# Accumulating the output products before normalizing, in the same step of an attention and MLP block

## The chip, the cores and the metric

The kernel runs on one core of one Trainium2 chip. The metric is the device time of one execution, in microseconds (us). The engines of the core are TensorE (PE: matrix products, with weight loads shown as PEld), VectorE (DVE), ScalarE (ACT), GpSimd (POOL) and SyncE (SP, which issues most DMAs). Each runs its own instructions in the order in which the program issues them; they wait for one another by semaphores.

## What is computed

One transformer block with modulated layer norms, in float32. The part that matters:

```python
h = _layernorm(x) * (1 + ca) + sa
# A: attention over the last W = 512 cached keys, 32 query heads, 16 kv heads
q = h @ wq
scores = einsum("bhqd,bhkd->bhqk", q, k) * Dh ** -0.5
o = einsum("bhqk,bhkd->bhqd", softmax(scores), v)
x = x + ga * (o @ wo)
h = _layernorm(x) * (1 + cb) + sb
# B: MLP
x = x + gb * ((silu(h @ w1) * (h @ w3)) @ w2)
```

There are 2048 rows of x, a width of 576, a head size of 128 and an MLP width of 4608.

## The kernel before

Each float32 operand of a product is split into two float16 halves, high and low, and a product is made of three: high by high, high by low, low by high. The MLP uses a fast scheme with seven products in place of eight; its weights are made ready in the background during the attention stage, by small tasks with due times.

**Slots.** The attention stage is a loop over 128 slots `i`, one for each pair of a query head and a block of 512 rows, and inside it over four tiles `t` of 128 rows. A slot's work is spread over several passes of the loop. In pass `i`, at tile `t`, the program issues:

- `scores(i, t)`: three products (L483) into a bank `pss`; VectorE then takes the maximum (L487) and scales it (L488) for ScalarE's exponential, `weights(i, t)` (L500), whose end frees the bank;
- `turn_away`, `half_high` and `half_low`: the exponentials of tiles 0 to 2 are split by ScalarE (L532) and GpSimd (L537) and turned by a transposing DMA (L544). Tile 3 is turned on TensorE instead (`turn`, L523), and its halves come from ScalarE (`turn_high`, L527, at t = 1 of the next pass) and VectorE (`turn_low`, L552, at t = 2);
- `query(i + 1, t)`: a third of the next slot's query products (L410, L414), which ScalarE (L467) and VectorE (`query_low`, L473) split;
- after the four tiles, `values(i - 1)`: twelve products (L562) of the turned weights with the values. The first two need only high halves of the weights, the third needs the low half of all four tiles.

**Normalizing.** `normalize(i - 2)` (L571) is one VectorE instruction at t = 1. It multiplies the value products `po` by the reciprocals of the row sums `r`, which arrive by DMA, into a buffer `on` that shares three places with other tiles. `split_on(i - 2)` makes its halves at t = 3 (L581 on ScalarE, L582 on GpSimd).

**Output products.** Two slots (the two query heads of one kv head) make a pair. `attend_out(pair, t, j, ...)` multiplies the outputs of one tile by the output weights: six products (L433) for j = 0, six more for j = 1, into one accumulator `E`, two PSUM banks wide and single. With j = 1, VectorE adds the result to the running rows (`acc`, L592, "the accumulate"). The table `outs` lays these out one call a tile, so that in the steady state the call with j = 1, and its accumulate, falls on t = 1 and t = 3 of each pass, and the first products of the next result (j = 0) on t = 2 and t = 0.

**Small sums in E.** The background tasks find peaks of weights. A tiny product (L310, L1135, L1167) sums a peak over partitions into columns 400 to 415 of E's second bank, and a small VectorE copy takes it out (L315, L1141, L1170). These are the tasks `("total", t)` and `("taken", t)` of a step; totals are issued just ahead of the accumulate, copies after it, on odd steps.

**Order.** The schedule is manual: on every engine the instructions run in program order. At t = 1, VectorE therefore has the maximum and its scaling, normalize, the accumulate, copies if any, the step's tasks (peak searches such as L305, L1126 and L1162, gates, statistics), and then the next tile's maximum and turn_low.

**Factors of activations.** `act_factors(lo, hi, piece)` (L1180) turns peaks of weights into the scale factors of the MLP's activations, in five pieces of a few instructions on at most 28 columns, called once near the end of the attention stage and once early in the MLP stage, one piece a step.

Of the kernel before, what the change touches and what calls it, by code (L numbers as in the profile page):

```python
# [38 lines left out]
G = NF // 2  # L39
# [9 lines left out]
def tile_block(  # L49
# [35 lines left out]
    def t_bank():  # L85
        return tpool.tile([P, 512], F32, tag="T", name="pt")

    def half_split(a):
        return a.rearrange("p (a n) -> p a n", a=2)
# [338 lines left out]
    def back(ps, o, w, t, first, last):  # L428

        rows = slice(t * P, (t + 1) * P)  # L430
        for n, (x, y) in enumerate(((0, 0), (0, 1), (1, 0))):
            for h in range(2):
                nc.tensor.matmul(  # L433
                    ps[:, h, :HALF],
                    o[:, x, rows],
                    w[:, y, h * HALF : (h + 1) * HALF],
                    start=first and n == 0,
                    stop=last and n == 2,
                )
# [11 lines left out]
    n = len(slots)  # L451
# [19 lines left out]
    def query_low(i):  # L471
        q, ps = state[i]["qT"], state[i].pop("q")
        nc.vector.scalar_tensor_tensor(q[:, 1], ps, Q_DOWN, q[:, 0], op0=ALU.mult, op1=ALU.subtract)  # L473
# [43 lines left out]
    def turn(i, t):  # L517

        st = state[i]
        p = st.pop(("p", t))  # L520
        ps = st["t"] = t_bank().rearrange("p (j n) -> p j n", j=KC)
        for j in range(KC):
            nc.tensor.transpose(ps[:, j, :], p[:, j * P : (j + 1) * P], ident)  # L523
# [5 lines left out]
    def half_high(i, t):  # L529

        hp = state[i]["hp", t] = pool.tile([P, 2, SB], F16, tag="hf", name="hp", bufs=HF)
        nc.scalar.copy(hp[:, 0, :], state[i]["p", t])  # L532

    def half_low(i, t):

        hp = state[i]["hp", t]
        nc.gpsimd.tensor_sub(hp[:, 1, :], state[i].pop(("p", t)), hp[:, 0, :])  # L537

    def turn_away(i, t):

        if t == 0:
            state[i]["pt"] = pool.tile([P, 2, KC, SB], F16, tag="pt", name="ptw")
        pt = state[i]["pt"]
        nc.sync.dma_start_transpose(  # L544
            out=pt.rearrange("p x c n -> p (x c) n")[:, :, t * P : (t + 1) * P],
            in_=state[i].pop(("hp", t)).rearrange("p x k -> p (x k)"),
        )

    def turn_low(i, t):
        cols = slice(t * P, (t + 1) * P)  # L550
        pt = state[i]["pt"]
        nc.vector.tensor_sub(pt[:, 1, :, cols], state[i]["t"], pt[:, 0, :, cols])  # L552
# [14 lines left out]
    def normalize(i):  # L567
        st = state[i]
        po = st.pop("po")
        on = st["on"] = pool.tile([P, SB], F32, tag="raw", name="on", bufs=RB)  # L570
        nc.vector.tensor_mul(  # L571
            on.rearrange("d (t p) -> d t p", t=ST),
            po.rearrange("d (t p) -> d t p", t=ST),
            st["r"].rearrange("d p t -> d t p"),
        )
# [8 lines left out]
    def attend_out(pair, t, j, total):  # L584
        u, _, b = slots[2 * pair]
        lane[0] += j == 0
        ps = spare()
        back(ps, state[2 * pair + j]["o"], wos[u][:, j], t, j == 0, j == 1)
        if j == 1:
            run(*total)  # L590
            a = half_split(acc[b][:, t, :])
            nc.vector.scalar_tensor_tensor(  # L592
                a, ps[:, :, :HALF], factors[:, uses[u][0], 2:3], a, op0=ALU.mult, op1=ALU.add
            )
# [453 lines left out]
    def at(i, t, task, *args):  # L1048

        tasks.setdefault((i, t), []).append((task, args))  # L1050

    def run(i, t):
        for task, args in tasks.pop((i, t), ()):
            task(*args)
# [20 lines left out]
    def scale_cols(kind, ps, small, down):  # L1075

        nc.tensor.matmul(ps[:, :P], ones, spreads.pop(kind)[:, :P], start=True, stop=True)
        nc.vector.tensor_reduce(small[:, 2:3], ps[:, :P], axis=AX.X, op=ALU.max)
        powers(small, small[:, 2:3], 0, 1, 5, down)
        for v in (vecs["shift", kind], vecs["gain", kind]):  # L1080
            nc.vector.tensor_scalar(v, v, small[:, 10:11], None, op0=ALU.mult)
# [27 lines left out]
    out_down, acts_down = table[:, 2 * NF : 2 * NF + G + 1], table[:, 2 * NF + G + 1 : 2 * NF + 2 * G + 2]  # L1109
# [8 lines left out]
    def spare():  # L1118
        return lane[1][lane[0] % 2] if lane[1] else E
# [60 lines left out]
    def act_factors(lo, hi, piece):  # L1180

        top, h_down = mlp_small[:, 2:3], mlp_small[:, 5:6]
        both = stats.rearrange("p (g j) k -> p g j k", j=2)[:, lo:hi]
        downs, pairs = both[:, :, :, 0], both[:, :, :, 1]
        a = acts_down[:, lo:hi]
        if piece == 0:
            nc.vector.tensor_max(a, pairs[:, :, 0], pairs[:, :, 1])
            nc.vector.tensor_scalar(a, a, top, 2.5 * D * 2.0**-13.5, op0=ALU.mult, op1=ALU.mult)
        elif piece == 1:
            nc.vector.tensor_scalar(a, a, top, 2.0**-60, op0=ALU.mult, op1=ALU.max)  # L1190
            d = in_down[:, 2 * lo : 2 * hi]
            nc.vector.tensor_scalar(d, d, h_down, None, op0=ALU.mult)
        elif piece < 4:
            j = piece - 2
            nc.vector.reciprocal(pairs[:, :, j], a)
            nc.vector.tensor_mul(pairs[:, :, j], pairs[:, :, j], downs[:, :, j])
        else:
            if hi == G:
                hi += 1
                nc.vector.tensor_copy(acts_down[:, G : G + 1], acts_down[:, G - 1 : G])  # L1200
            d = out_down[:, lo:hi]
            nc.vector.tensor_scalar(d, d, mlp_gate_down, None, op0=ALU.mult)
            nc.vector.tensor_mul(d, d, acts_down[:, lo:hi])

    def find(into, u, k, *key):
# [52 lines left out]
    def step_at(step, task, *args):  # L1258
        at(step // ST, step % ST, task, *args)
# [78 lines left out]
    def late_at(step, task, *args):  # L1338
        at(("m", step // len(ORDER)), step % len(ORDER), task, *args)

    turns = len(items[ITEMS:]) // 4
    for late in range(turns):
# [15 lines left out]
            plan += [(step, make, number + k, maker, w, k), (step + STORE, store_now, number + k)]  # L1358
        for step, task, *args in plan:
            late_at(total + step, task, *args)  # L1360
    for piece in range(5):
        late_at(2 * len(ORDER) * turns + len(ORDER) + 1 + piece, act_factors, (NF - FEW) // 2, G, piece)
    for k, (i, t) in enumerate(((n - 4, 0), (n - 4, 2), (n - 3, 0), (n - 2, 0))):
        at(i, t, load_wset, 0, k)
# [81 lines left out]
    for c in range(3):  # L1446
        i = 117 + 3 * c
# [47 lines left out]
    at(109, 2, make_cols, "gain", "b", 4, 1.0, "T")  # L1495
    at(109, 3, lambda: spread_peaks("b", mlp_small))
    at(110, 1, lambda: scale_cols("b", t_bank(), mlp_small, 2.0**-8))
    for piece in range(5):
        step_at(ST * (n - 4) + 2 + piece, act_factors, 0, (NF - FEW) // 2, piece)
    for b in (2, 3):  # L1500
        for t in range(ST):
# [62 lines left out]
    for i in range(n + 2):  # L1564
        run(i, -1)
        for t in range(ST):
            if t > 1 and i < n:
                turn_away(i, t - 2)
            if t == 0 and 1 <= i <= n:
                turn_away(i - 1, 2)  # L1570
            slot, tile = (i - 1 if t == 1 else n, ST - 1)
            if 0 <= slot < n:
                turn(slot, tile)
            if i < n:
                scores(i, t)
            if 2 <= i <= n and t == 1:
                normalize(i - 2)
            if 1 <= i <= n and t == 2:
                turn_low(i - 1, ST - 1)
                if i == n:  # L1580
                    turning.close()
                    after = ctx.enter_context(tc.tile_pool(name="after", bufs=1, space=PSUM))
                    lane[1] = (E, after.tile([P, 2, 512], F32, tag="T2", name="pf"))
            if t == 3 and i + 1 < n:
                query_low(i + 1)
            if i < n:
                weights(i, t)
            if t < 3 and i < n:
                half_high(i, t)
                half_low(i, t)  # L1590
            if t == 1 and 1 <= i <= n:
                turn_high(i - 1, ST - 1)
            if 1 <= i <= n and t < 2:
                sums(i - 1, t)
            if 2 <= i <= n and t == 3:
                split_on(i - 2)
            if i + 1 < n and t < ST - 1:
                query(i + 1, t)
            if i >= m0:
                for _ in range(3 if (i, t) == (n + 1, 0) else 1):  # L1600
                    next(stream)
            for piece in outs.get((i, t), ()):
                attend_out(*piece, (i, ("total", t)))
            run(i, ("total", t))
            run(i, ("taken", t))
            run(i, t)
            if 1 <= i <= n and t == 2:
                sums(i - 1, t)
            run(i, t)
        if 1 <= i <= n:  # L1610
            values(i - 1)
        if i == n:
            normalize(n - 1)
            split_on(n - 1)
# [73 lines left out]
```

## Time and profile before

| | us |
|---|---|
| three runs | 2758.09, 2758.36, 2758.54 (median 2758.36) |
| profiled execution, its own time | 2758.39 |
| span of its instructions | 2756.2 |
| attention with running slots, window 97 to 1622: PE busy | 1495.1 of 1525.0 |
| same window: DVE, ACT, POOL busy | 1170.9, 1137.4, 1188.9 |
| MLP, window 1622 to 2757: PE busy | 1123.4 of 1135.0 |

The mean granted TensorE clock is 0.995. Busy time is the union of an engine's instructions; an engine that waits for a semaphore is idle. In the lines of the trace, `L592` is line 592 of the kernel, `acc<-pe,factors,acc` names what an instruction writes and reads, `[1.01 <-POOL o L582]` is idle time before it and what ended it. The rows of time are: start in us from the span's start, duration in us, engine, line, operation, tiles, shapes, count.

### The profile page before, as it was taken

The numbers are of one execution on the slowest core, as the hardware profiler recorded it, in microseconds if no ns is written. First come the engines' busy times: TensorE is split into PE (matmuls) and PEld (weight loads), VectorE is DVE, ScalarE is ACT, GpSimd is POOL, SyncE is SP. The second block draws the span as 40 slices with busy tenths as digits, with TensorE's granted clock in tenths as the row PEclk, the third lists the DMA queues.
The fourth block names the chain that finished last, engine by engine and source line by source line (L and its number), as shares of the span: only waits on it lengthen the run. The fifth ranks groups of instructions, "written<-read, shape, count | busy, mean of one in ns | idle before, by whom it ended". The sixth has DMA issues, their size and how long they took to land. (4 is left out here: it accounts for less than half of the span.)

```text
span 2756.2 us, 44751 instructions
## 1 busy us (share of the span) xinstructions
PE 2685.1 (97%) x15406; PEld 1512.8 (55%) x15406; DVE 1997.3 (72%) x3555; ACT 1617.8 (59%) x3013; POOL 1881.1 (68%) x1748
## 2 busy tenths in 40 slices
PE   6899999999999999999999999999999999999998
PEld 3455555555555555555555555555555555555555
DVE  7877788877788787877876667777766656666666
ACT  5777778777777877777677735544443333333332
POOL 5577788888788977877669637688873465333435
PEclk8999999999999999999999999999999999999999
DMA  5778888778786887989889945656643444333332
GB/s 186 171 178 193 194 182 188 175 176 189 169 185 166 190 196 180 214 181 210 192 189 208 256 131 171 200 167 200 210 149 108 161 121 128 103 102 111 104 107 87
DMA packets 593460, 463.84 MB, mean 168 GB/s; under 512 B 442704, under 2 KB 472528, under 8 KB 592208
## 3 DMA queue, kind: packets, MB, share of 16 engines
q1 hardware_dynamic: 592944, 460.69, 65.5%
q8 instruction: 121, 1.98, 0.3%
q14 instruction: 107, 0.88, 0.1%
q10 hardware_dynamic: 288, 0.30, 0.0%
HBM read 264.19 MB, written 95.99 MB: 131 GB/s over the span
## 5 line engine op out<-in xcount | busy, mean ns | idle before, releaser
L537 POOL TENSOR_TENSOR hp<-p,hp 128x512 f16<-128x512 f32 x384 | 449.6, 1173 | 266.3 <-ACT hp L532 143.8
L500 ACT ACTIVATE p<-pss,table,factors 128x512 f32<-128x512 f32 x512 | 396.9, 775 | 354.9 <-DVE table L488 182.5
L849 PEld LDWEIGHTS <-wset 128*128 128x128 f16 x3528 | 344.5, 98 | 337.4 <-issue 4.4
L487 DVE TENSOR_REDUCE table<-pss 128x1 f32<-128x512 f32 x512 | 350.5, 685 | 206.0 <-PE pss L483 202.0
L849 PE MATMUL py<-hset,wset 128*128 128x512 f16 x2016 | 483.1, 380 | 0.0
L433 PE MATMUL pe<-o 128*128 128x288 f16 x3024 | 453.1, 286 | 10.1 <-DVE acc L592 9.6
L483 PE MATMUL pss<-k,qT 128*128 128x512 f16 x1536 | 418.8, 380 | 14.2 <-ACT p L500 10.4
L433 PEld LDWEIGHTS <-o 128*128 128x128 f16 x3072 | 300.5, 98 | 184.5 <-issue 15.7
L562 PE MATMUL po<-ptw,v 128*128 128x512 f16 x1536 | 358.2, 381 | 8.2 <-DMA ptw<-hp 4.1
L849 PE MATMUL px<-hset,wset 128*128 128x512 f16 x1512 | 361.5, 379 | 1.6 <-ACT p L500 1.6
L94 POOL TENSOR_TENSOR akv<-u,akv 128x512 f16<-128x512 f32 x141 | 165.0, 1180 | 179.2 <-ACT akv L93 171.4
L410 PE MATMUL pq<-hT,wq 128*128 128x512 f16 x1092 | 282.3, 381 | 1.8 <-POOL hT L252 1.1
L532 ACT CAST hp<-p 128x512 f16<-128x512 f32 x384 | 237.3, 618 | 13.2 <-POOL hT L256 0.6
L562 PEld LDWEIGHTS <-v 128*128 128x128 f16 x1536 | 147.8, 98 | 172.8 <-issue 16.2
L483 PEld LDWEIGHTS <-qT 128*128 128x128 f16 x1536 | 147.8, 98 | 129.2 <-issue 15.5
L934 PEld LDWEIGHTS <-akv 128*128 128x128 f16 x1728 | 169.0, 98 | 89.3 <-issue 0.8
L592 DVE SCALAR_TENSOR_TENSOR acc<-pe,factors,acc 128x576 f32<-128x576 f32 x252 | 204.6, 812 | 4.3 <-PE pe L433 4.3
L582 POOL TENSOR_TENSOR o<-on,o 128x512 f16<-128x512 f32 x128 | 150.3, 1174 | 54.0 <-ACT o L581 51.9
L410 PEld LDWEIGHTS <-wq 128*128 128x128 f16 x1092 | 107.2, 98 | 128.5 <-issue 2.9
L928 DVE SCALAR_TENSOR_TENSOR acc<-pf,table,acc 128x576 f32<-128x576 f32 x140 | 113.5, 811 | 80.8 <-PE pf L934 80.8
L1027 ACT COPY u<-py 128x512 f32<-128x512 f32 x72 | 42.2, 586 | 202.1 <-PE py L849 200.2
L1020 ACT ACTIVATE s<-s,table 128x512 f32<-128x512 f32 x72 | 52.0, 722 | 176.3 <-DVE s L1019 176.3
(246 smaller groups left out, 4793.8 us busy)
## 6 DMA issues: line engine op xcount, KB each, us to landing
wset<-wd SPq DMA_DIRECT2D x213, 320.0 KB, 3.2
r<-row SPq DMA_DIRECT2D x128, 256.0 KB, 3.9
oset<-od SPq DMA_DIRECT2D x106, 288.0 KB, 3.2
wraw<-in_w SPq DMA_DIRECT2D x36, 768.0 KB, 5.4
wd<-wmade SPq DMA_DIRECT2D x75, 320.0 KB, 3.3
wset<-wd SPq DMA_DIRECT2D x71, 160.0 KB, 2.2
w2raw<-in_w SPq DMA_DIRECT2D x19, 576.0 KB, 5.2
wd<-ring SPq DMA_DIRECT2D x33, 320.0 KB, 2.9
```

The lines of the kernel that those rows point to most:

```text
L94: eng.tensor_sub(halves[:, 1], src, halves[:, 0])
L410: nc.tensor.matmul(ps, w[:, k // 2, m, :], hT[:, DC + m if k == 1 else m, :], start=s == 0, stop=False)
L433: nc.tensor.matmul(ps[:, h, :HALF], o[:, x, rows], w[:, y, h * HALF : (h + 1) * HALF], start=first and n == 0, stop=last and n == 2,)
L483: nc.tensor.matmul(pss, q[:, x, rows], k[:, y, :], start=n == 0, stop=n == 2)
L487: nc.vector.tensor_reduce(nm[:, 0:1], pss, axis=AX.X, op=ALU.max, negate=True)
L500: nc.scalar.activation(p, pss, AF.Exp, bias=nm[:, 1:2], scale=factor, accum_out=st["l"][:, t : t + 1])
L532: nc.scalar.copy(hp[:, 0, :], state[i]["p", t])
L537: nc.gpsimd.tensor_sub(hp[:, 1, :], state[i].pop(("p", t)), hp[:, 0, :])
L562: nc.tensor.matmul(po, v[:, x, c, :], pt[:, y, c, :], start=c == 0 and n == 0, stop=c == KC - 1 and n == 2)
L592: nc.vector.scalar_tensor_tensor(a, ps[:, :, :HALF], factors[:, uses[u][0], 2:3], a, op0=ALU.mult, op1=ALU.add)
L849: nc.tensor.matmul(ps, w[:, a, :], h[:, b, :], start=start and n == 0, stop=stop and n == 6, skip_group_check=True)
L934: nc.tensor.matmul(ps[:, h, :HALF], a[:, rows], w[:, b, :], start=m == 0, stop=m == 2)
```

## The change

Two things change. First, at t = 1 the call of `normalize(i - 2)` moves within the same step: from right behind the scores to behind the step's `attend_out` calls. On VectorE it thus goes from ahead of the accumulate to behind it, still ahead of the copies ("taken") and of the step's tasks. Second, the last piece of `act_factors` is cut in two, so that its final product comes one step later; the two places that schedule the pieces count to six.

```diff
         elif piece < 4:
...
-        else:
+        elif piece == 4:
             if hi == G:
                 hi += 1
                 nc.vector.tensor_copy(acts_down[:, G : G + 1], acts_down[:, G - 1 : G])
             d = out_down[:, lo:hi]
             nc.vector.tensor_scalar(d, d, mlp_gate_down, None, op0=ALU.mult)
+        else:
+            hi += hi == G
+            d = out_down[:, lo:hi]
             nc.vector.tensor_mul(d, d, acts_down[:, lo:hi])
...
-    for piece in range(5):
+    for piece in range(6):
         late_at(2 * len(ORDER) * turns + len(ORDER) + 1 + piece, act_factors, (NF - FEW) // 2, G, piece)
...
-    for piece in range(5):
+    for piece in range(6):
         step_at(ST * (n - 4) + 2 + piece, act_factors, 0, (NF - FEW) // 2, piece)
...
             if i < n:
                 scores(i, t)
-            if 2 <= i <= n and t == 1:
-                normalize(i - 2)
             if 1 <= i <= n and t == 2:
...
             for piece in outs.get((i, t), ()):
                 attend_out(*piece, (i, ("total", t)))
+            if 2 <= i <= n and t == 1:
+                normalize(i - 2)
             run(i, ("total", t))
             run(i, ("taken", t))
             run(i, t)
```

## The prediction

> **What bounds the kernel now.** First the page: busy time by engine.
>
> ```profile
> PE 2685.1 (97%) x15406; PEld 1512.8 (55%) x15406; DVE 1997.3 (72%) x3555; ACT 1617.8 (59%) x3013; POOL 1881.1 (68%) x1748
> ```
>
> TensorE (PE) is the bound; its idle time is 2756.2 - 2685.1 = 71 us. VectorE (DVE) has slack on average, but the change touches only steps of the attention stage, so the second view is who TensorE waited for (us in total, times, longest):
>
> ```profile
> PE pe L433 <- DVE acc L592: 9.6, 10, 2.4
> ```
> ```profile
> PE po L562 <- DVE ptw L552: 3.2, 7, 0.7
> ```
> L433 are the output products into the one accumulator E; L592 reads E out ("accumulate"); L552 (turn_low) makes the low half of the turned weights of tile 3, which the third value product (L562) of the same slot needs; L315, L1141 and L1170 are small copies of peaks out of a corner of E. Third, the VectorE and TensorE timelines of the longest of the ten waits (start us, us, engine, line, what; in brackets the idle time before and who ended it):
>
> ```profile
> 581.83 1.06 DVE L571 TENSOR_TENSOR on<-po,r 128x512 f32<-128x512 f32 x1 [2.94 <-DMA r<-row]
> 582.80 0.81 DVE L592 SCALAR_TENSOR_TENSOR acc<-pe,factors,acc 128x576 f32<-128x576 f32 x1
> 583.53 0.68 DVE L305 TENSOR_REDUCE top<-kvraw 128x1 bf16<-128x512 f32 x1
> ```
> ```profile
> 583.67 0.90 PE L433 MATMUL pe<-o 128*128 128x288 f16 x6 [2.43 <-DVE acc L592]
> ```
>
> The multiplication L571 (normalize) waited 2.94 us for its DMA, and the accumulate, whose products were long complete, stood behind it; TensorE then waited for E. All ten waits are of this kind, at t = 1 (the others mostly await a buffer). The change removes this order.
>
> **What the swap does to an ordinary step.** Most steps look like this one:
>
> ```profile
> 1000.44 0.21 DVE L488 TENSOR_SCALAR table<-table,factors 128x1 f32<-128x1 f32 x1
> 1000.57 1.09 DVE L571 TENSOR_TENSOR on<-po,r 128x512 f32<-128x512 f32 x1
> 1001.57 0.82 DVE L592 SCALAR_TENSOR_TENSOR acc<-pe,factors,acc 128x576 f32<-128x576 f32 x1
> 1002.29 0.69 DVE L487 TENSOR_REDUCE table<-pss 128x1 f32<-128x512 f32 x1
> 1003.02 0.21 DVE L488 TENSOR_SCALAR table<-table,factors 128x1 f32<-128x1 f32 x1
> 1003.20 0.69 DVE L552 TENSOR_TENSOR ptw<-pt,ptw 128x512 f16<-128x512 f32 x1
> ```
> ```profile
> 1000.59 0.90 PE L433 MATMUL pe<-o 128*128 128x288 f16 x6
> ...
> 1002.84 0.90 PE L433 MATMUL pe<-o 128*128 128x288 f16 x6
> ...
> 1004.96 2.75 PE L562 MATMUL po<-ptw,v 128*128 128x512 f16 x12
> ```
>
> VectorE is ready at 1000.57, while TensorE completes E only at 1000.59 + 0.90 = 1001.49. Today the multiplication fills just that hole. Swapped, the accumulate cannot start before 1001.49: VectorE idles 0.92 us, is free 0.72 later (1002.29 - 1001.57) at 1002.21, and the multiplication holds it for another 1.00 (1001.57 - 1000.57) to 1003.21 instead of 1002.29. **All that is queued behind it on VectorE comes 0.92 later**: the maximum of tile 2, L552, and any small copies and peak searches of the step. E itself is free earlier by 0.08 only, and TensorE wanted it at 1002.84 anyway. Here it costs nothing: L552 would end at 1004.81, and the third value product starts two spacings of some 2.75/12 = 0.23 after 1004.96, at 1005.4: 1.5 us of slack before, 0.6 after. Most slots of the VectorE timeline have this hole. Normalize issues this one instruction and no DMA, so the queues of SP and GpSimd keep their order; its reader, split_on, comes two tiles later, and the bank of po that it frees is written again by the next slot's value products only.
>
> **Term 1, the waits that go.** Eight of the ten go whole: 9.6 - 2.43 - 2.01 = 5.2 us. The long ones are the wait at 583.67 and this one, behind which the windows view (stretch, its length, busy time of each engine, granted clock, DMA share, GB/s) has a stretch at half clock:
>
> ```profile
> 966.32 0.90 PE L433 MATMUL pe<-o 128*128 128x288 f16 x6 [2.01 <-DVE acc L592]
> ```
> ```profile
> 967.80:971.00 3.20, 3.20 (x14) 1.57 (x13) 2.43 (x6) 2.30 (x5) 0.69 (x1) 0.50 1.54 144
> ```
>
> At 581.83 the multiplication still waits for its DMA, so what follows comes only the accumulate's 0.73 (583.53 - 582.80) earlier. TensorE, freed 2.43 earlier, is stopped again by L552, which is late next: 0.7 is kept. At 966.32, 3.20 us at a granted clock of 0.50 are a loss of 1.6 that goes too; of these 3.6 about 1.6 is kept, for the same reason (0.7, and 0.9 that the half clock cost before L552 was asked for). Term 1: -(5.2 + 0.7 + 1.6) = **-7.5** (if all were kept: -11.2).
>
> **Term 2, the small copies out of E.** In 36 of the steps a copy stands behind the accumulate, first and last:
>
> ```profile
> 109.36 0.15 DVE L315 COPY us<-pe 128x1 f32<-128x1 f32 x1
> ```
> ```profile
> 1461.08 0.15 DVE L1170 COPY table<-pe 128x1 f32<-128x1 f32 x1
> ```
> ```profile
> 436.67 1.08 DVE L571 TENSOR_TENSOR on<-po,r 128x512 f32<-128x512 f32 x1
> 437.67 0.82 DVE L592 SCALAR_TENSOR_TENSOR acc<-pe,factors,acc 128x576 f32<-128x576 f32 x1
> 438.40 0.15 DVE L1141 COPY table<-pe 128x2 f32<-128x2 f32 x1
> ```
> ```profile
> 436.69 0.90 PE L433 MATMUL pe<-o 128*128 128x288 f16 x6
> ...
> 438.99 0.90 PE L433 MATMUL pe<-o 128*128 128x288 f16 x6
> ```
>
> The copy is issued by the step's "taken" tasks, which the multiplication now precedes. New order: E complete 437.59, accumulate, multiplication at 438.32, copy at 439.32 to 439.47. Does the next output product wait for the copy? It reads other columns of E, and whether it must can be seen where a copy comes late:
>
> ```profile
> 1170.36 0.17 DVE L315 COPY us<-pe 128x1 f32<-128x1 f32 x1
> ```
> ```profile
> 1170.59 0.90 PE L433 MATMUL pe<-o 128*128 128x288 f16 x6 [0.18 <-DVE us L315]
> ```
>
> The product starts 0.06 after the copy's end: it waits. So at 438.99 it would start at 439.52, 0.54 late. By the same working 29 of the 36 steps lose 0.5 to 0.6 (0.56 on average, 16.2) and seven, where VectorE has little or no hole, 1.0 together: **+17.2**. Below, if copies do not hold TensorE: 0.
>
> The Trainium skill's page "PSUM — Partial Sum Buffer" (section "PSUM bank collisions raise a hardware error") says that two engines' accesses are to be ordered by bank and quadrant, not by address, even for disjoint columns; by that rule the copies hold the product and the sum keeps this term, while by addresses alone it would end 17.2 lower. The row at 1170.59 agrees with the rule.
>
> **Term 3, L552 late.** With a reduction or two between accumulate and L552, the slack of the step at 1000 is gone:
>
> ```profile
> 391.32 1.35 DVE L1162 TENSOR_REDUCE peak_cols<-w2raw 128x1 bf16<-128x1152 f32 x1
> ...
> 393.43 0.68 DVE L552 TENSOR_TENSOR ptw<-pt,ptw 128x512 f16<-128x512 f32 x1
> ```
> ```profile
> 394.17 2.32 PE L562 MATMUL po<-ptw,v 128*128 128x512 f16 x10 [0.15 <-DVE ptw L552]
> ```
>
> L552 already ends (394.11) where TensorE waits for it, so the whole 0.93 becomes a wait. Taking 0.93 less the slack in each step without a copy (and less what L552 itself waits for ScalarE): five steps have none left (4.6), five have 0.3 to 0.65 (2.6), eight about 0.7 (2.0), eight nearly enough (0.5): 9.7. The L552 of the first and the last of these 26:
>
> ```profile
> 212.04 0.68 DVE L552 TENSOR_TENSOR ptw<-pt,ptw 128x512 f16<-128x512 f32 x1
> ```
> ```profile
> 1558.05 0.68 DVE L552 TENSOR_TENSOR ptw<-pt,ptw 128x512 f16<-128x512 f32 x1
> ```
>
> In the copy steps, already held 0.55, another 2.5. Term 3: **+12.2**.
>
> **Other.** Exponentials of tile 2 come up to 0.9 later, hence the buffers of the scores that they release, the qT halves and the transposing DMAs behind them. The nearest row:
>
> ```profile
> PE pss L483 <- ACT p L500: 10.4, 15, 2.5
> ```
>
> If these 15 waits grow by half of 0.92 each, 7 us come on top; if TensorE, held elsewhere in the same steps, finds half of them done, 5 go. I take 0, between the two. The sixth piece only moves a product of a few columns one step on, twice:
>
> ```profile
> L1203 DVE TENSOR_TENSOR table<-table 128x5 f32<-128x5 f32 x1 | 1.2, 1194 | 0.0
> ```
>
> Nothing reads it so soon; VectorE's own slack there hides it (between -1.2 and +1.2 without that cover): 0.
>
> **Sum.** -7.5 + 17.2 + 12.2 = +21.9. The profiled execution took 2758.39 us (its span 2756.2 and 2.2 around it), 0.03 from the median of 2758.36: **2780.3**, say 2780.
>
> **Rivals.** (a) *Faster*: VectorE's idle share covers the hole and only the waits go. That needs L552 to have over 0.93 us of slack nearly everywhere and copies that do not hold E: 2758.4 - 11.2 = 2747. For it: 28% idle VectorE, and 1.5 us of slack in the step at 1000. Against: 394.17 and 1170.59. The Trainium skill's "Perfetto Trace Analysis" (section "Optimization Strategy") advises to find what the busiest engine's gaps wait for and to start that sooner; followed blindly it gives this rival. (b) *Copies free*: the product at 1170.59 was held by something that ended with the copy. Then 2758.4 - 7.5 + 12.2 = 2763. (c) *No change in effect*: holes and waits cancel, within 2753 to 2763; needs half of term 3 absorbed as well as (b). (d) *Worse*: the chain behind the later exponentials adds its 7, 2787 and over.
>
> **Chances.** Forecast 0.70, (a) 0.08, (b) 0.12, (c) 0.05, (d) 0.05. A measurement tells 0.2% (5.5 us) from no change. (b) lies at that edge: 0.07 within, 0.05 slower. Slower 0.70 + 0.05 + 0.05 = 0.80, same 0.05 + 0.07 = 0.12, faster 0.08. The range runs from (b), 2763, to (d), 2788.
>
> **What would show it.** Right: waits of L433 for L592 nearly gone; new waits of L433 for L1141, L1170 and L315, some 30 of half a us; waits of L562 for L552 up from 3.2 to about 12; VectorE idling before L592 for TensorE, many times the 4.3 of today:
>
> ```profile
> DVE acc L592 <- PE pe L433: 4.3, 3, 3.0
> ```
>
> Wrong: L433 starting before the copy has ended (term 2), or L552 no later relative to the value products (term 3).

## The result, and the profile after

The changed kernel takes 2784.08 us (median of five runs, 2783.5 to 2789.65) against 2758.54 for the kernel before on the same chip: a ratio of 1.0095, 95% interval 1.0081 to 1.0109. That is 25.5 us slower by the medians and 26.2 (22.3 to 30.1) by the ratio, which is not that of the medians. The prediction was 2780, 21.9 slower than its base.

The profiled execution of the changed kernel took 2789.65 us, 5.6 above its median; its rows are read as what happens, and sizes are taken from the timed runs. The page, span and busy time by engine:

```profile
span 2787.8 us, 44802 instructions
...
PE 2694.9 (97%) x15406; PEld 1512.9 (54%) x15406; DVE 1998.9 (72%) x3555; ACT 1617.7 (58%) x3013; POOL 1877.4 (67%) x1748
```

TensorE runs the same 15406 products and is the bound as before. The windows view of the two kernels, each with the attention stage to its last output product and with the rest (stretch, its length, busy time of PE, PEld, DVE, ACT and POOL, granted clock, DMA share, GB/s), before:

```profile
97.00:1622.00 1525.00, 1495.14 (x8592) 839.72 (x8590) 1170.91 (x2355) 1137.42 (x2202) 1188.91 (x1126) 1.00 0.82 189
1622.00:2756.00 1134.00, 1123.38 (x6527) 637.72 (x6525) 752.56 (x1041) 423.90 (x710) 638.97 (x562) 1.00 0.44 139
```

and after:

```profile
97.00:1655.90 1558.90, 1505.61 (x8590) 840.25 (x8588) 1173.45 (x2355) 1136.93 (x2201) 1185.33 (x1126) 1.00 0.81 184
1655.90:2787.80 1131.90, 1121.71 (x6527) 637.07 (x6525) 751.52 (x1040) 423.84 (x710) 638.66 (x562) 1.00 0.44 139
```

The attention stage grew by 33.9 us, the rest shrank by 2.1: all of the loss is made where the instructions were swapped. That PE's busy time grows by 10.5 with the same products is in part a matter of reading. Neighbouring rows of PE overlap by some 0.16 us (below, 443.00 + 0.90 = 443.90, while its successor in the trace starts at 443.74), and a row that had to wait doesn't, so each wait is some 0.1 to 0.16 longer than the idle time in its row. The stage has 82 rows that waited where it had 42, which makes 4 to 6 of the 10.5; the rest stays open.

Whom TensorE waited for after (us in total, times, longest):

```profile
PE po L562 <- DVE ptw L552: 13.3, 23, 1.8
PE pss L483 <- ACT p L500: 11.8, 13, 2.5
PE pe L433 <- DVE table L1141: 6.1, 15, 0.5
PE pe L433 <- DVE us L315: 5.5, 12, 0.5
...
PE pe L433 <- DVE table L1170: 2.2, 5, 0.5
```

The row of 9.6 us in which L433 waited for L592 is gone. In its place stand 32 waits of L433 for the small copies, none over 0.5, together 13.8, and every one of these products starts 0.05 to 0.06 after the copy's end; and the waits of L562 for L552 rose from 3.2 to 13.3. Whom VectorE waited for after:

```profile
DVE acc L592 <- PE pe L433: 75.4, 87, 3.2
...
DVE acc L592 <- PE pe L1135: 11.8, 13, 0.9
DVE acc L592 <- PE pe L310: 11.8, 13, 0.9
...
DVE acc L592 <- PE pe L1167: 2.7, 3, 0.9
```

The hole before the accumulate, three waits and 4.3 us before, is now met 87 times for L433, and 29 times more where the small sum is the last product into E. The copy step that the prediction worked out (436.67 to 438.99 before), now on VectorE and on TensorE:

```profile
443.98 0.82 DVE L592 SCALAR_TENSOR_TENSOR acc<-pe,factors,acc 128x576 f32<-128x576 f32 x1 [0.92 <-PE pe L1135]
444.72 1.07 DVE L571 TENSOR_TENSOR on<-po,r 128x512 f32<-128x512 f32 x1
445.70 0.16 DVE L1141 COPY table<-pe 128x2 f32<-128x2 f32 x1
```
```profile
443.00 0.90 PE L433 MATMUL pe<-o 128*128 128x288 f16 x6
...
445.92 0.90 PE L433 MATMUL pe<-o 128*128 128x288 f16 x6 [0.45 <-DVE table L1141]
```

VectorE idles 0.92, the copy ends at 445.86, and 0.06 later the next output product starts: 2.92 after the one before it, where it was 2.30 (436.69 to 438.99). That is 0.62 late; the prediction had 0.54. And the third value product of the step that stood at 394.17, with no slack; the output product ahead of it before, then the same product and the value product after:

```profile
391.27 0.90 PE L433 MATMUL pe<-o 128*128 128x288 f16 x6
```
```profile
396.62 0.90 PE L433 MATMUL pe<-o 128*128 128x288 f16 x6
...
400.49 2.32 PE L562 MATMUL po<-ptw,v 128*128 128x512 f16 x10 [0.75 <-DVE ptw L552]
```

In its row the wait grows from 0.15 to 0.75. Counted from that output product it starts 3.87 later instead of 2.90 (391.27 to 394.17): 0.97 late, where the prediction had 0.93. The row understates it, since the small sum ahead of it (L1167) came late too, without a row of its own.

### The profile page after: what moved, and what is told of

Its sections match the earlier page's. It is cut to its first block, busy times and chain, and to the rows that moved or that the text cites. A ratio compares the mean times of both kernels' runs of the same rounds, so it can differ in the third digit from the quotient of the medians.

```text
span 2787.8 us, 44802 instructions
## 1 busy us (share of the span) xinstructions
PE 2694.9 (97%) x15406; PEld 1512.9 (54%) x15406; DVE 1998.9 (72%) x3555; ACT 1617.7 (58%) x3013; POOL 1877.4 (67%) x1748
## 5 line engine op out<-in xcount | busy, mean ns | idle before, releaser
L500 ACT ACTIVATE p<-pss,table,factors 128x512 f32<-128x512 f32 x512 | 396.9, 775 | 386.5 <-DVE table L488 220.4
L433 PE MATMUL pe<-o 128*128 128x288 f16 x3024 | 453.2, 286 | 13.9 <-DVE table L1141 6.1
L483 PE MATMUL pss<-k,qT 128*128 128x512 f16 x1536 | 418.5, 380 | 15.5 <-ACT p L500 11.8
L433 PEld LDWEIGHTS <-o 128*128 128x128 f16 x3072 | 300.9, 98 | 192.3 <-issue 23.7
L562 PE MATMUL po<-ptw,v 128*128 128x512 f16 x1536 | 364.0, 382 | 23.4 <-DVE ptw L552 13.3
L592 DVE SCALAR_TENSOR_TENSOR acc<-pe,factors,acc 128x576 f32<-128x576 f32 x252 | 204.8, 813 | 102.3 <-PE pe L433 75.4
L562 PEld LDWEIGHTS <-v 128*128 128x128 f16 x1536 | 147.8, 98 | 194.5 <-issue 36.4
L483 PEld LDWEIGHTS <-qT 128*128 128x128 f16 x1536 | 148.1, 98 | 130.4 <-issue 16.8
```

What stands on the lines that cost most here:

```text
L433: nc.tensor.matmul(ps[:, h, :HALF], o[:, x, rows], w[:, y, h * HALF : (h + 1) * HALF], start=first and n == 0, stop=last and n == 2,)
L483: nc.tensor.matmul(pss, q[:, x, rows], k[:, y, :], start=n == 0, stop=n == 2)
L500: nc.scalar.activation(p, pss, AF.Exp, bias=nm[:, 1:2], scale=factor, accum_out=st["l"][:, t : t + 1])
L562: nc.tensor.matmul(po, v[:, x, c, :], pt[:, y, c, :], start=c == 0 and n == 0, stop=c == KC - 1 and n == 2)
L592: nc.vector.scalar_tensor_tensor(a, ps[:, :, :HALF], factors[:, uses[u][0], 2:3], a, op0=ALU.mult, op1=ALU.add)
```

## The experiments

The question was not whether these waits exist but what each is worth, and whether the terms of the sum are independent. Each kernel was timed beside the kernel before on its chip; its time against before is (ratio - 1) x 2758.4, with the interval of the ratio. The trace of the changed kernel shows 124 swapped steps: 36 with a copy, the 26 of term 3, the ten waits and 52 others (texts below that were written before their runs count 53 of these). The edits choose in which steps normalize goes behind the accumulate, by a condition `last`:

```diff
-            if 2 <= i <= n and t == 1:
+            last = ...
+            if 2 <= i <= n and t == 1 and not last:
                 normalize(i - 2)
...
             for piece in outs.get((i, t), ()):
                 attend_out(*piece, (i, ("total", t)))
+            if 2 <= i <= n and t == 1 and last:
+                normalize(i - 2)
```

| kernel | normalize behind the accumulate in | median us | ratio, 95% interval | us against before |
|---|---|---|---|---|
| copy_steps | the 36 steps with a copy | 2777.16 | 1.007, 1.0057 to 1.0084 | +19.3 |
| plain_steps | all steps without one | 2767.66 | 1.0033, 1.0021 to 1.0045 | +9.1 |
| copies_first | all, and behind the copies too | 2780.28 | 1.0077, 1.0064 to 1.0091 | +21.2 |
| copy_behind | the copy steps, behind the copies too | 2770.82 | 1.005, 1.0038 to 1.0062 | +13.8 |
| late_low | the 26 steps of term 3 | 2769.92 | 1.0046, 1.0034 to 1.0058 | +12.7 |
| ten_waits | the ten steps whose wait goes | 2756.33 | 0.9992, 0.9984 to 1.0001 | -2.2 |
| free_steps | the 52 other plain steps | 2763.21 | 1.0022, 1.0012 to 1.0032 | +6.1 |
| free_early | 23 of these | 2760.14 | 1.0007, 0.9998 to 1.0015 | +1.9 |
| free_late | 29 of these | 2762.08 | 1.0018, 1.0009 to 1.0026 | +5.0 |
| tile_earlier | the ten; elsewhere a tile earlier | 2759.9 | 1.001, 1.0002 to 1.0019 | +2.8 |
| pieces_only | none; the sixth piece alone | 2756.54 | 0.9999, 0.9991 to 1.0008 | -0.3 |

**Copy steps alone**, `last = (i, ("taken", 1)) in tasks`:

> Normalize behind the accumulate only in the steps that have a copy out of E (36 with running output products); the factors stay in five pieces. Theory (three terms: waits that go, copies that hold TensorE, turn_low late): only the copy steps pay, 17.2 for the late copies and 2.5 for turn_low, no wait goes: 2758.5 + 19.7 = 2778. Rival (copies are free, the hole in VectorE costs the same in every step): 36 of 122 steps pay 36/122 of the 25.5 us measured, 2766.

+19.3. Its waits:

```profile
PE pe L433 <- DVE acc L592: 9.4, 10, 2.4
PE pe L433 <- DVE table L1141: 6.4, 15, 0.5
PE pe L433 <- DVE us L315: 5.5, 12, 0.5
PE po L562 <- DVE ptw L552: 5.3, 12, 0.7
...
PE pe L433 <- DVE table L1170: 2.5, 5, 0.6
```

All of the copies' waits are here, with the ten old ones still in place. The size is that of term 2 and the copy steps' share of term 3 (17.2 + 2.5).

**Steps without a copy alone**, `last = (i, ("taken", 1)) not in tasks`:

> Normalize behind the accumulate only in the steps without a copy; five pieces. Theory: -7.5 for the waits of the accumulate that go, +9.7 for turn_low late: 2761, with no wait of L433 for a copy beyond those of before. Rival (copies free): 86 of 122 steps pay 18 us, 2776.

+9.1, well over the +2.2 expected. Whether the ten waits give back less or the other steps cost more, this run alone can't tell; the later ones ask for each part.

```profile
PE po L562 <- DVE ptw L552: 10.5, 17, 1.8
```

**Copies ahead of normalize.** If the copies are what costs, taking them out of normalize's way should give most of it back:

```diff
             run(i, ("total", t))
             run(i, ("taken", t))
+            if 2 <= i <= n and t == 1:
+                normalize(i - 2)
             run(i, t)
```

> The changed kernel, but with normalize behind the copies too, still ahead of the step's other tasks: E is free right after accumulate and copy. Theory: the 17.2 us of the copies go, turn_low in those steps has less cover and takes back up to 3: 2784 - 17.2 + 0 to 3 = 2767 to 2770; waits of L433 for copies below 1 us. Rival (copies free): nothing changes, 2784.

A miss: +21.2 (17.7 to 25.1), only 5.0 less than the change's 26.2, where some 15 were expected. The copies' waits are gone, but

```profile
PE po L562 <- DVE ptw L552: 19.4, 30, 1.8
PE pss L483 <- ACT p L500: 14.5, 19, 2.5
```

L552, which the prediction had late by 2.5 us in the copy steps, is now late in many of them. So the terms are not independent: while a copy holds TensorE, VectorE gets on towards L552. To price that by itself, the same in the copy steps only:

> Only the 36 copy steps are swapped, and in them the multiplication goes behind the accumulate and the small copies. Theory: the copies no longer hold the next output product (its 33 waits for L1141, L315 and L1170, 20.4 us worked out from TensorE's timeline when these steps alone were swapped, go to none), but L552 now shows its whole delay: 0.93 less its slack adds up to some 10 us in these steps instead of the 2.5 that were left beside the held product. So about +10 against before, 2769, of which the hold is worth some 9 of the +18 that these steps cost with the copies behind. Rival one: L552 alone is not late enough, and taking the copies out of the way frees nearly all: +2.5, 2761. Rival two: the later exponentials that follow from the hole, not the copies, are what costs: as slow as with the copies behind, 2777, with waits for L500 above 14 us.

+13.8 against +19.3 with the copies behind: the hold is worth 5.5, near the 5.0 of the pair before (26.2 - 21.2), though in both pairs the intervals overlap, and most of the rest is L552, whose row was 3.2 in the kernel before:

```profile
PE po L562 <- DVE ptw L552: 12.1, 19, 1.0
```

The expectation, which put some 10 on L552, comes nearest of the three. One step shows the exchange. With normalize ahead of the copy, TensorE and then VectorE:

```profile
456.28 0.90 PE L433 MATMUL pe<-o 128*128 128x288 f16 x6 [0.46 <-DVE us L315]
...
458.39 2.32 PE L562 MATMUL po<-ptw,v 128*128 128x512 f16 x10
```
```profile
458.02 0.68 DVE L552 TENSOR_TENSOR ptw<-pt,ptw 128x512 f16<-128x512 f32 x1
```

and with the copy first:

```profile
457.55 1.24 PE L562 MATMUL po<-ptw,v 128*128 128x512 f16 x5 [0.87 <-DVE ptw L552]
```
```profile
456.81 0.68 DVE L552 TENSOR_TENSOR ptw<-pt,ptw 128x512 f16<-128x512 f32 x1
```

In the first the output product waits 0.46 for the copy and L562 for nothing; in the second nothing holds the output product, and L562 starts 0.06 after L552's end at 457.49, having waited 0.87.

**The 26 steps of term 3 alone,** `last` by a list of their passes:

> Normalize behind the accumulate only in the 26 steps without a copy in which turn_low was reckoned to come late; five pieces. Theory (each step costs 0.93 less its slack): 9.7 over the kernel before, 2759 + 10 = 2769. Rival (the hole in VectorE costs the same in every step, 25.5 / 122 = 0.21): 2759 + 5.4 = 2764.5.

+12.7, on the theory's side. Its waits for L552:

```profile
PE po L562 <- DVE ptw L552: 8.3, 13, 1.8
```

These rows grew by 5.1, less than the time, since they leave out short waits and the overlap. The length of a pass doesn't: from the start of the first value product (L562) at the end of one pass to that at the end of the next. Its usual length is the median over the profiles in which neither this pass nor the one before was changed. The 26 passes and those right behind them, without the ten waits' passes and those right behind these, are 41; together they took 11.5 us longer than usual here, near the 9.7 of the theory, and 10.9 in plain_steps.

**The ten waits alone,** `last = i in (6, 36, 37, 44, 68, 69, 76, 84, 121, 124)`:

> Normalize behind the accumulate only in the ten steps in which TensorE waited for the accumulate before; five pieces. Theory: the waits go, of the two long ones 0.7 and 1.6 us are kept: 2758.5 - 7.5 = 2751. Rival (what TensorE is freed from it meets again at turn_low or at the transposing DMA in all ten): 2758. Second rival (all 9.6 and the stretch at half clock are kept): 2747.

-2.2 (-4.4 to +0.3), a miss. The waits are gone and most of the time isn't. Two of the small ones first, of passes 36 and 37. The value products that end passes 35 to 38, before and here:

```profile
476.63 2.75 PE L562 MATMUL po<-ptw,v 128*128 128x512 f16 x12
488.92 2.75 PE L562 MATMUL po<-ptw,v 128*128 128x512 f16 x12
501.28 2.75 PE L562 MATMUL po<-ptw,v 128*128 128x512 f16 x12
513.32 2.80 PE L562 MATMUL po<-ptw,v 128*128 128x512 f16 x12
```
```profile
476.01 2.75 PE L562 MATMUL po<-ptw,v 128*128 128x512 f16 x12
487.59 2.87 PE L562 MATMUL po<-ptw,v 128*128 128x512 f16 x12
499.32 2.93 PE L562 MATMUL po<-ptw,v 128*128 128x512 f16 x12
511.93 2.80 PE L562 MATMUL po<-ptw,v 128*128 128x512 f16 x12
```

Pass 36 is 0.71 shorter (12.29 to 11.58) and that is kept. Pass 37 is 0.63 shorter (12.36 to 11.73), but pass 38 is 0.57 longer (12.04 to 12.61), in pieces too short for a row. Passes 68 to 70 repeat this, and pass 7 gives back what pass 6 gains. Where the longest went is seen in its step, first before and then here. TensorE before:

```profile
580.64 0.59 PE L414 MATMUL pq<-hT,wq 128*128 128x512 f16 x2
583.67 0.90 PE L433 MATMUL pe<-o 128*128 128x288 f16 x6 [2.43 <-DVE acc L592]
...
588.72 0.81 PE L483 MATMUL pss<-k,qT 128*128 128x512 f16 x3
```

TensorE with the ten waits gone, and VectorE:

```profile
579.15 0.59 PE L414 MATMUL pq<-hT,wq 128*128 128x512 f16 x2
...
583.03 0.18 PE L1135 MATMUL pe<-peak_cols 128*128 128x2 bf16 x1 [1.17 <-DMA ptw<-hp]
...
584.47 3.94 PE L562 MATMUL po<-ptw,v 128*128 128x512 f16 x10 [0.73 <-DVE ptw L552]
588.20 0.92 PE L483 MATMUL pss<-k,qT 128*128 128x512 f16 x3
```
```profile
582.03 0.95 DVE L1126 TENSOR_REDUCE peak_cols<-wraw 128x1 bf16<-128x768 f32 x1
```

From the same L414 to the same L483 it took 8.08 us before and 9.05 now. TensorE ran into the next two results of VectorE: the small sum L1135 needs the peaks of L1126, which end at 582.98 (the row names a DMA, but the product starts 0.05 behind L1126, which makes its input), and then L552. And the ten value products took 3.94, where ten took 2.32 at 400.49 above. The windows view shows why, here and before:

```profile
584.50:587.70 3.20, 3.20 (x9) 1.17 (x9) 2.46 (x6) 3.17 (x8) 1.58 (x2) 0.58 1.23 178
```
```profile
583.60:588.60 5.00, 4.80 (x29) 2.68 (x29) 4.23 (x9) 2.56 (x6) 1.62 (x2) 1.00 1.19 201
```

The granted clock is 0.58 behind the two short waits, where it was 1.00 behind the single long one. This is one execution: passes 44 and 45 together take 26.12 us before and 27.21 here, but 24.94 in plain_steps and 24.64 in the changed kernel. The other long wait went as hoped: from the L414 to the L483 around it 9.02 us before (963.72 to 972.74), 6.92 now (962.55 to 969.47), the half-clock stretch gone with it.

**The other 52 plain steps:**

> Normalize behind the accumulate only in the other steps without a copy, where turn_low was reckoned to have the slack, and without the ten in which the accumulate waited; five pieces. Theory: nothing, 2759 (up to 2763 if the later exponentials hold transposing DMAs and score buffers). Rival (same cost in every step): 50 of 122 steps, 2769.

+6.1 in the median, though its profile, of an execution of 2758.16, is 5 us below that and shows little of it. So they were split into halves:

> The 53 steps without a copy, without one of the ten waits and without a late L552 cost +6 when all were swapped, with no wait to show for it. Here only the 23 of them up to slot 66 are swapped. If the cost is a small one in each step, this gives +2.6, 2760; if it is made in a few steps, this and the other half come out unequal, and the profile of the dearer half has a wait that before does not have; if it is no cost of these steps but how runs of one kernel scatter, both halves lie within 0.1% of before.

> The other 30 of those 53 steps, behind slot 66. If the cost is a small one in each step, +3.4, 2761; if it is made in a few steps, one half has all of the 6 and its profile a wait that before does not have; if it is scatter, within 0.1% of before.

+1.9 and +5.0, together about the 6.1. Both profiles are near their medians (2760.14 and 2760.26). They speak against a small cost in each step: over the swapped passes the median change of a pass's length is 0.00 in each half. Three passes do grow. In the early half, and in every run that swaps these steps but in no other, pass 9 is 0.47 and pass 11 0.79 longer; TensorE waits there for ScalarE (0.30 and 0.69):

```profile
PE pt L240 <- ACT hf L251: 3.1, 3, 2.1
```

Before, this row has only the one wait of 2.1. In the late half it is the last pass, 128, where the output products wait for the halves that `split_on` makes of the normalized slot, before and here:

```profile
1596.89 1.64 PE L433 MATMUL pf<-o 128*128 128x288 f16 x12 [1.04 <-DVE ptw L552]
```
```profile
1598.97 1.64 PE L433 MATMUL pf<-o 128*128 128x288 f16 x12 [1.99 <-ACT o L581]
```

That is 0.95 more. These three make 2.2 of the 6.1. The rest stays open: it lies in no pass that these profiles show as regularly longer.

**Elsewhere a tile earlier.** To keep VectorE's hole filled and still let the ten waits go, normalize was put at the end of t = 0, except in the ten steps:

```diff
             run(i, t)
+            if 2 <= i <= n and t == 0 and not last:
+                normalize(i - 2)
```

> Normalize a tile earlier (end of t = 0), where VectorE idles ahead of the next maximum, except in the ten steps in which it waited, where it stands behind the accumulate; five pieces. Theory: the hole before the accumulate is then real idle time, but accumulate, copy and turn_low come no later than before, so nothing new waits and turn_low's own waits shrink: 2759 - 2 (the ten) - 3 = 2754. Rival (the row sums or a buffer have not come by then, VectorE stalls ahead of the maximum and the exponentials come late): 2765 and over.

+2.8, a miss. The multiplication now stands ahead of the next maximum, and

```profile
PE pss L483 <- ACT p L500: 15.4, 15, 3.8
```

which is 10.4 before, took back more than the ten waits gave: TensorE waited longer for the exponentials to free the buffers of the scores. The rival had the mechanism, at a smaller price: the waits of the multiplication for its row sums rose from 5.5 to 24.6 us.

**The sixth piece alone:**

> Only the sixth piece of the factors; normalize where it was before. Theory: two VectorE instructions of a few columns move one step: 0, 2759. Rival (it matters): any ratio whose interval leaves 1.

-0.3 (-2.5 to +2.2): nothing, as expected. No kernel tried is surely faster than the one before; the ten steps alone come nearest.

## Why the prediction was right, point by point

**Direction and size.** Slower, 2784 against 2780, inside the range. Each of the four signs named for it appeared: in the changed kernel L433 no longer waits for L592; 32 waits of half a us for the copies ("some 30"); L562 for L552 at 13.3 ("about 12"); and a hole before the accumulate of 75.4 us, where it was 4.3.

**The hole.** 0.92 worked out from one step; the trace has it in the steps shown, and the delay that follows is 0.62 at the copy (0.54 predicted) and 0.97 at the value product without slack (0.93 predicted).

**Term 1, -7.5: mis-sized.** The ten steps alone give -2.2 (-4.4 to +0.3). Of the two long waits the prediction kept 0.7 and 1.6. The second gave 2.10; the first lost 0.97 in ten_waits, to L1126, L552 and the half clock. In the changed kernel, where the multiplication waited 0.47 for its DMA and not 1.35 as in ten_waits, the same stretch (589.71 to 596.30) took 6.59, a gain of 1.49. What was wrong is that eight waits "go whole": the prediction asked what is late next for the two long ones only. Of the five small waits that are alike in every execution, those of passes 6, 37 and 69 give back in the next pass nearly all of the 0.5 to 0.7 that they gain, and those of 36 and 68 keep 0.7 each: 1.5 us in all, where their rows had 2.8. The passes of the other five (44, 76, 84, 121, 124) scatter; pass 44 took 13.13 to 15.89 in executions that did not change it. With them, the ten passes and those right behind are 2.6 us shorter than usual in ten_waits, 5.2 in the changed kernel and 7.0 in plain_steps. So a single execution can come near the 7.5, and the median of eleven doesn't.

**Term 2, +17.2: right for the change.** With its 2.5 of term 3 it was 19.7, and the copy steps measured 19.3 (15.7 to 23.2). The condition behind it, that a small copy out of other columns of E holds the next product, is shown for this program: in all 32 cases the product starts 0.05 to 0.06 after the copy's end, and with the copies first those waits are gone. Whether the chip would need the wait, no run shows: every kernel here keeps it. But 17.2 is not what the copies are worth by themselves. Taken out of the way they give back 5.5 (19.3 - 13.8, the two intervals overlap), since L552 is late behind them.

**Term 3, +12.2: about right.** Its 9.7 in the steps without a copy measured 12.7 (9.4 to 16.0), 11.5 by the passes' lengths. Its 2.5 in the copy steps holds as long as the copies hold TensorE, and not otherwise.

**Other, 0.** The waits of L483 for L500 grew by 1.4 (10.4 to 11.8), within the bounds. The 52 steps that were to cost nothing cost 6.1 (3.3 to 8.8), which no term had; 2.2 of it are waits for ScalarE in three passes.

**The sum.** The copy steps and the others, timed apart, come to 19.3 + 9.1 = 28.4, near the change's 26.2. The three parts of the others come to 12.7 - 2.2 + 6.1 = 16.6, and together they measured 9.1 (5.8 to 12.4). The uncertainties of the four, added as squares, are some 6 us, and the gap is 7.5: either chance, or parts that partly pay for the same thing. The profiles point to chance: the late passes cost 11.5 in late_low and 10.9 in plain_steps, so they are not cheaper in company, while the ten waits differ by 4.4 between the two profiles, in passes that scatter. With one profile for each kernel this isn't shown. The near hit of the total (3.6 off) is luck in part: term 1 was some 5 too good by the timed run, and a loss of some 6 came from steps that were held free, in parts that add up to more than the whole.

**The rivals.** (a), faster, falls: copies hold the product, and L552 has no slack in many steps. (b), free copies, falls with copy_steps. (c), no effect, falls with the time. (d), later exponentials, has 1.4 of its 7 in its row. The waits of L562 for anything but L552, among them those for the transposing DMAs, are 8.9 us in the changed kernel and 4.4 before, but 8.7 in ten_waits too, where only ten steps moved; so more of (d) is not shown.

## What to carry to other kernels

On an engine that works in order, an instruction that is ready may be filling the hole in front of one that isn't; before the two are swapped, work out when the second's input is complete, and follow everything queued behind, small copies included. A wait that is removed is worth what the next late thing leaves of it, and that holds for the half-us waits as for the long ones: of five, three came back in the next pass. Two delays that spring from the same hole hide one another: the price of each has to be measured with the other gone as well as with it there.

## What was not expected of the hardware

The granted clock fell to 0.58 for 3.2 us behind two waits of 1.17 and 0.73 us that lay 0.7 apart, and to 0.50 behind a single one of 2.01 us, but stayed at 1.00 behind a single one of 2.43: the length of a wait alone did not decide it in these runs. The 23 executions of the kernel before that ran beside the last three kernels lie between 2753.58 and 2762.83 us, so a single profile can be off by as much as the ten waits are worth.
